# Sinkhorn attention, Fourier mixing and MLP on one core: V routed through DRAM, memsets between loads, exp-ln norms, and unread matmuls in planned gaps

## The chip, the cores and the metric

One core of one Trainium2 chip. The metric is device time in microseconds (us) from the first to the last instruction of one launch, as the runs list it (about 1.7 us more than the span in the profile). Engines: PE = TensorE, PEld = its weight load, DVE = VectorE, ACT = ScalarE, POOL = GpSimd, SP = SyncE. A run is called slow when it is over 1.5% above the fastest of its kernel; verdicts use fast runs.

## The reference

```python
P = sort_net                                   # [4, 8, 8, 8]
for _ in range(5):                             # Sinkhorn
    P = exp(P - P.max(-1)); P /= P.sum(-1); P /= P.sum(-2)
k_sorted = einsum('bhij,bhjcd->bhicd', P, k_blocks)   # 8 blocks of 96 keys
v_sorted = einsum('bhij,bhjcd->bhicd', P, v_blocks)
attn = softmax(q_block @ k_sorted_block.T / 8)        # block by block
x = (attn @ v_sorted_block) -> [4, 768, 512]
u = x + real(fft(fft(x, axis=1), axis=2))
un = (u - mean(u)) / sqrt(var(u) + 1e-6)
out = u + relu(un @ w1) @ w2                          # 512 -> 2048 -> 512
```

## The kernel before

The program is a list of operations with priorities and estimated durations. A planner turns it into one fixed order for each engine before the kernel is built. At run time an engine takes its instructions in that order and stands at one whose semaphore has not come. "Batch" is one of the four batches, and V0 and V1 are the halves of V that serve batches 0 and 1, and 2 and 3. g = 0, 1 are the two halves of a batch's rows. AV is the matmul of the attention weights with V, FF1 that with w1, FF2 that with w2.

Loads and memsets at the start:

```python
for n in range(4):                                  # exp(scores) buffers
    P.add({"POOL": (1.5, 1.6)}, lambda _, n=n: nc.gpsimd.memset(
        eb4[0:96, n, :], 0.0), w=[("ebz", n)], prio=-190.0)
load_qk("k", 0, 0, -5000.0); load_qk("q", 0, 0, -4999.0)
load_v(0, 0, -4998.0);       load_v(0, 1, -4997.0)
load_qk("k", 0, 1, -4996.0); load_qk("q", 0, 1, -4995.0)
...                                                 # the rest later
```

V's path, on the chip alone: sum over a block by PE, copies into a tile ordered by d, 64 small mixing matmuls with keys on the output's partitions, strided evacuation:

```python
for hf in range(2): ...  nc.tensor.matmul(psm.ap, idh, nat[t][...512...])
for n in range(8):       # t == 0: copy;  t == 1: subtract the block mean
    copy(e, vcx[d, r, c], nat[t]["p (c r) d -> p d r c"])
for n in range(16):
    for dd in range(4):
        nc.tensor.matmul(o, vcx[:, 96*d:96*d+m], bd, start=True, stop=(t == 1))
        ...
    copy(e, vsb[0:96, :, 4*n:4*n+4], ps["p (d g) -> p g d"])
```

The norm, and the rows of u, in six buffers (three for each g):

```python
many("u", 6, [128, DM], F32)
G.tensor_scalar(var, var, 1e-6, op0=add)            # G = GpSimd
G.tensor_tensor(ny, var, mhalf, op=pow)
G.tensor_tensor(nm, mean, ny, op=mult); G.tensor_scalar(nm, nm, -1.0, ...)
# dft2: u = RSC * x + mixed      (VectorE writes a buffer of u)
# ff2 : u = ff2 bank + u         (VectorE), then the store frees the buffer:
P.add({"SP": (0.1, 2.3)} if g == 0 else {"POOL": (1.2, 3.5)}, store_u, ...)
```

The two figures of the store are the planner's: how long the engine is held, and when the result is there.

The softmax here doesn't subtract the row's maximum and nothing guards it: scores larger than these inputs give would overflow.

Of the kernel before, what the change touches and what calls it, by code (L numbers as in the profile page):

```python
# [18 lines left out]
D = 64  # L19
NB = 8  # L20
# [7 lines left out]
LOOK = {}  # L28
QB = (2, 3)
# [14 lines left out]
GT = 384  # L44


def _consts():
# [56 lines left out]
    vrow = np.zeros((1, 128, D + 1), f16)  # L104
# [9 lines left out]
    def as32(m):  # L114
# [8 lines left out]
                rows=rows, erow=np.tile(erow, (1, 4)), vrow=vrow, pack=pack)  # L123


class Op:
    __slots__ = ("n", "costs", "fn", "preds", "succs", "left", "ready", "prio",
                 "vts", "fresh", "nbytes", "end", "start", "eng", "tag",
                 "crit", "late")
# [13 lines left out]
class Plan:  # L143
# [14 lines left out]
    def add(self, costs, fn, r=(), w=(), prio=None, nbytes=0, tag="",  # L158
            after=()):
# [7 lines left out]
        o.preds, o.succs, o.vts, o.fresh = set(after), [], [], []  # L167
        for k in r:
            o.preds.update(self.wr.get(k, ()))
# [41 lines left out]
    def schedule(self):  # L211
# [48 lines left out]
        while todo:  # L260
# [70 lines left out]
            for s in o.succs:  # L331
                s.left -= 1
                for x in s.costs:
                    s.ready[x] = max(s.ready[x],
                                     o.end + (0.03 if x == e else self.XL))
                if s.left == 0:
                    for x in s.costs:
                        avail[x].append(s)
# [27 lines left out]
def kernel(  # L366
# [22 lines left out]
    def many(name, n, shape, dtype):  # L389
# [18 lines left out]
    vcx = ct("vcx", [128, 128 * D + 2], F16)  # L408
    dtab = vcx[:, 6144:7168].rearrange("p (c w) -> p c w", c=4)
    lt = vcx[0:97, 7168:7168 + LTW]  # L410
    vsf = ct("vsf", [97, 128 * (D + 1)], F16)
    vsb = vsf[:, 0:128 * (D + 1)].rearrange("p (g w) -> p g w", w=D + 1)
    eb4 = ct("eb4", [97, 4, EW], F16)
    P.pool("eb", [eb4[:, n, :] for n in range(4)])
# [14 lines left out]
    many("un", 2, [128, DM], F16)  # L429
# [9 lines left out]
             vcx[:, 7938:8194].bitcast(F32).rearrange(  # L439
# [7 lines left out]
    mhalf = ct("mhalf", [128, 3], F32)  # L447
    mone = ct("mone", [128, 3], F32)
# [7 lines left out]
    pk = hr[1].rearrange("p a b -> p (a b)")[0:32, 0:1024].rearrange(  # L456
        "p (i x) -> p i x", i=NB)
    pv = hr[1].rearrange("p a b -> p (a b)")[0:32, 1024:3072].bitcast(
        F32).rearrange("p (i x) -> p i x", i=NB)
    pws = hr[1].rearrange("p a b -> p (a b)")[0:32, 3072:3232].bitcast(F32)  # L460
# [9 lines left out]
    def load(dst, src, nbytes, w, prio, eng="POOL", r=(), after=()):  # L470
        e = {"POOL": nc.gpsimd, "SP": nc.sync}[eng]
        c = (0.8, 0.8) if eng == "POOL" else (0.1, 2.3)
        o = P.add({eng: c}, lambda _: e.dma_start(dst, src), r=r, w=w,  # L473
                  prio=prio, nbytes=nbytes, tag="load", after=after)
        o.late = 4.0 if after else 0.0
        return o


    slot = {}
# [34 lines left out]
    def load_v(t, hf, prio):  # L514
        load(nat[t].rearrange("p (c d) -> p c d", d=D)[
            :, 48 * hf:48 * hf + 48, :],
            vv[128 * t:128 * t + 128, 48 * hf:48 * hf + 48, :], 1572864,
            [("nat", t, hf)] + (hk(0)[8 * hf:8 * hf + 8] if t == 0 else
                                kqk(2 * hf) + kqk(2 * hf + 1)), prio)
# [10 lines left out]
    for n in range(4):  # L530
        P.add({"POOL": (1.5, 1.6)}, lambda _, n=n: nc.gpsimd.memset(
            eb4[0:96, n, :], 0.0), w=[("ebz", n)], prio=-190.0, tag="ebz")
    for n in range(2):
        t_ = P.pools["ks"][n][2]
        P.add({"POOL": (0.4, 0.5)}, lambda _, t_=t_: nc.gpsimd.memset(
            t_[:, :, 96:128], 0.0), w=[("ksz", n)], prio=-195.0, tag="ksz")
    P.add({"POOL": (0.6, 0.7)}, lambda _: nc.gpsimd.memset(
        vsb[0:96, :, D:D + 1], 1.0 / XSC), w=["vsz"], prio=-200.0, tag="vsz")
    P.add({"POOL": (0.1, 0.4)}, lambda _: nc.gpsimd.memset(
        pmt[:, 4:7, DM:DM + 2], 0.0), w=["pmz"], prio=-150.0, tag="small")  # L540
    for t_, val in ((negone, -1.0), (mhalf, -0.5), (mone, 1.0)):
        P.add({"POOL": (0.1, 0.4)}, lambda _, t_=t_, val=val:
              nc.gpsimd.memset(t_, val), w=["smalls"], prio=-199.0, tag="small")
    P.add({"POOL": (0.9, 0.9)}, lambda _: nc.gpsimd.tensor_tensor(
        mone, mone, mhalf, op=ALU.pow), r=["smalls"], w=["mone"], prio=-198.0,
        tag="small")
# [5 lines left out]
            "o (n s) -> o n s", n=4), 13376),  # L552
        vrow=(vsf[96:97, 0:128 * (D + 1)], cn["vrow"].ap(), 16640),
# [14 lines left out]
    load_qk("k", 0, 0, -5000.0)  # L568
    load_qk("q", 0, 0, -4999.0)
    load_v(0, 0, -4998.0)  # L570
    load_v(0, 1, -4997.0)
    load_qk("k", 0, 1, -4996.0)
    load_qk("q", 0, 1, -4995.0)
    load_c("dtab", -4994.0)
    load_c("lt", -4993.0)
    load_c("cs", 19.0)
    load_c("tab", 20.0)
    for c in range(4):
        load_w1(c, 40.0 + c)
    for hf in range(2):  # L580
        load_qk("k", 1, hf, 30.0 + hf)
        load_qk("q", 1, hf, 30.5 + hf)
    for c in range(4):
        load_w2(c, 50.0 + c)
# [4 lines left out]
    V = nc.vector  # L589

    exps = []

    def sk(c, fn):
        o = P.add(c, fn, r=["pw", "rs"] + hk(1), w=["pw", "rs"], tag="sink")
        if "ACT" in c:
            exps.append(o)

    for it in range(5):
# [16 lines left out]
        sk({"DVE": (0.21, 0.21)}, lambda _: V.tensor_tensor(  # L615
# [6 lines left out]
        r=["pw"], w=["pk"] + hk(1), tag="pk")  # L622
    P.add({"ACT": (1.0, 1.05)}, lambda _: nc.scalar.copy(
        pv.rearrange("p i (g j) -> p i g j", j=NB),
        pw[:, :, None, :].broadcast_to([32, NB, 16, NB])),
        r=["pw"], w=["pv"] + hk(1), tag="pv")
# [6 lines left out]
    P.add(pe(0.45), f, r=["pk", "pack"] + hk(1), w=[bk], tag="psk")  # L633
# [35 lines left out]
    def v_path(t):  # L669
        n3 = nat[t].rearrange("p (c d) -> p c d", d=D)  # L670
        psm = Buf("pm", "pf") if t else Buf("pm")
        stage = [i for n in range(4) for i in kqk(n)] if t else hk(0)
        for hf in range(2):
            def f(_, hf=hf):
                for n in range(6):
                    nc.tensor.matmul(
                        psm.ap, idh,
                        nat[t][:, 3072 * hf + 512 * n:3072 * hf + 512 * n
                               + 512], start=(hf == 0 and n == 0),
                        stop=(hf == 1 and n == 5))  # L680
            P.add(pe(mm(512, 6) * (1.0 if t else 1.2)), f,
                  r=[("nat", t, hf), "pack"] + (
                      stage if t else stage[8 * hf:8 * hf + 8]), w=[psm], tag="psm")
        P.add({"DVE": (0.6, 0.68)}, lambda _: V.tensor_reduce(
            vb[:, 0, :], psm.ap.rearrange("p (c d) -> p d c", d=D),
            axis=AX.X, op=ALU.add), r=[psm], w=["vb"], tag="vb")
# [8 lines left out]
        vcd = vcx[:, 0:6144].rearrange("p (d r c) -> p d r c", r=6, c=16)  # L695
        for n in range(8):
            qd, hf = divmod(n, 2)
            dr = slice(16 * qd, 16 * qd + 16)
            src = n3[:, 48 * hf:48 * hf + 48, dr].rearrange(
                "p (c r) d -> p d r c", r=6)  # L700
            dst = vcd[:, dr, :, 8 * hf:8 * hf + 8]
            if t == 0:
                P.add({"DVE": dve(768), "ACT": act(768, 0.75)},
                      lambda e, dst=dst, src=src: copy(e, dst, src),
                      r=[("nat", 0, hf)] + stage[8 * hf:8 * hf + 8],
                      w=[("vcx", n)], tag="vcp")
            else:
                P.add({"DVE": dve(768, 1.0, 0.55)},
                      lambda _, dst=dst, src=src, dr=dr: V.tensor_tensor(  # L709
                          dst, src, vbn[:, dr, None, None].broadcast_to(  # L710
                              [128, 16, 6, 8]), op=ALU.subtract),
                      r=[("nat", 1, hf), "vbn"] + stage,
                      w=[("vcx", n)], tag="vcd")

    def v_mix(t):
        bd = bdv16[t].rearrange("p g i -> p (g i)")
        for n in range(16):
            ps = Buf("pm", "pf")

            def f(_, n=n, ps=ps):  # L720
                for dd in range(4):
                    d = 4 * n + dd
                    m = 96 if d == D - 1 else 128
                    o = ps.ap[0:m, 128 * dd:128 * dd + 128]
                    nc.tensor.matmul(o, vcx[:, 96 * d:96 * d + m], bd,  # L725
                                     start=True, stop=(t == 1))
                    if t == 0:
                        nc.tensor.matmul(  # L728
                            o, vbn[:, d:d + 1].broadcast_to([128, m]), bd,
                            start=False, stop=True)  # L730
            P.add(pe(0.46 if t == 0 else 0.24), f,
                  r=[("vcx", i) for i in range(2 * (n // 4), min(
                      8, 2 * ((4 * n + 4) // 16) + 2))] + [("bdv16", t)]
                  + (["vbn"] if t == 0 else []),
                  w=[ps], tag="vmix")
            P.add({"ACT": (0.68, 0.81), "DVE": (0.65, 0.8)},
                  lambda e, n=n, ps=ps: copy(
                      e, vsb[0:96, :, 4 * n:4 * n + 4],
# [651 lines left out]
```

## Time and profile before

| | before |
|---|---|
| median of 4 runs | 289.35 us (288.78 to 290.27) |
| first FF1 matmul | 72.14 us |
| last matmul ends | 282.39 us |
| TensorE's work: before, after the first FF1 | 39.1, 202.9 us |
| lost: before, after the first FF1 | 33.0, 7.4 us |

"Work" is the number of matmuls of each kind times their spacing in a dense stretch, and "lost" is the length of the stretch less the work. So a matmul at half clock counts as lost time too. Losses of stretches of 10 us, and sums of two of them, count the matmuls at their edges whole and read up to 0.4 us too low for each 10 us; sums over longer stretches are given as "some", corrected for that. Besides the lines that the prediction shows, three matter later. Timeline of VectorE and GpSimd (start, busy us, engine, line, instruction):

```profile
7.51 6.16 POOL L531 MEMSET eb<- 96x1672 f16 x4
12.95 1.28 DVE L661 COPY vcx<-hr 128x768 f16<-128x768 f16 x1
15.00 0.68 DVE L619 CAST hr<-hr 32x1024 f16<-32x1024 f32 x1
```

GpSimd's four memsets lie beside the Sinkhorn. One VectorE copy beside their end takes 1.28 us, and the one behind it 0.78. VectorE's waits after the first FF1 (waiting line, what released it, us in total, times, longest) hold one for a store of u, a short one:

```profile
DVE u L1161 <- DMA out_dram<-u: 0.3, 1, 0.3
```

### The profile page before, as it was taken

How to read it: one execution, taken by the hardware profiler on the slowest of the kernel's cores; microseconds unless marked ns; L12 is line 12 of the kernel's file. 1: busy time of each engine (PE TensorE's matmuls, PEld its weight loads, DVE VectorE, ACT ScalarE, POOL GpSimd, SP SyncE). 2: the span in 40 equal slices, each digit the busy share in tenths (PEclk: the TensorE clock that was granted, in tenths of full speed). 3: DMA queues.
4: the chain of work that ended last, by engine and by line, in shares of the span. 5: the costliest groups of instructions: out<-in, count | busy, mean ns of one | idle time of the engine just before them, and what ended most of it. 6: DMA issues, size and time to landing. Idle time of an engine off the chain costs nothing.

```text
span 288.2 us, 5805 instructions
## 1 busy us (share of the span) xinstructions
PE 261.6 (91%) x2284; PEld 155.7 (54%) x2284; DVE 171.5 (60%) x405; ACT 158.2 (55%) x323; POOL 67.7 (23%) x116
## 2 busy tenths in 40 slices
PE   0389988797999999999999999999999999999991
PEld 0247876554566566554566556445545545545540
DVE  4686999999999999850469853146114315310010
ACT  2676979886778946882269026416703614714600
POOL 8974300003920460020410000131100212200022
PEclk9995999999999999999999999999999999999997
DMA  7999999910992499412112011221221022032002
GB/s 111 214 264 244 213 208 208 221 35 16 97 169 39 64 165 146 97 21 38 73 50 46 13 73 38 45 86 48 41 91 36 10 48 109 12 66 76 14 9 101
DMA packets 42529, 26.33 MB, mean 91 GB/s; under 512 B 30106, under 2 KB 38824, under 8 KB 42500
## 3 DMA queue, kind: packets, MB, share of 16 engines
q0 software_dynamic: 23536, 18.31, 37.7%
q1 hardware_dynamic: 18966, 7.64, 11.5%
q8 instruction: 18, 0.29, 0.4%
q14 instruction: 9, 0.07, 0.1%
HBM read 28.96 MB, written 6.29 MB: 122 GB/s over the span
## 4 chain that ended last, share of the span: by engine, by line
PE 49%; DVE 24%; issue 16%; DMA 6%; POOL 4%; POOLq 0%; ACT 0%; DVEq 0%
PE bank L1275 19%; PE bank L1254 18%; DMA hr<-in_v_dram 4%; DVE vcx L709 3%; DVE vsf L661 3%; DVE rt L1007 2%; PE bank L992 2%; PE bank L1150 2%; PE bank L898 2%; DMA out_dram<-u 2%; DVE st L1187 1%; PE bank L953 1%; DVE eb L975 1%; DVE ks L661 1%; POOL out_dram L1298 1%
## 5 line engine op out<-in xcount | busy, mean ns | idle before, releaser
L1266 ACT ACTIVATE hr<-bank 128x384 f16<-128x384 f32 x115 | 56.3, 491 | 76.3 <-PE bank L1254 75.1
L1254 PE MATMUL bank<-ut,w1sb 128*128 128x384 f16 x512 | 91.5, 326 | 0.7 <-ACT ut L661 0.7
L1275 PE MATMUL bank<-w2sb,hr 128*128 128x512 f16 x384 | 87.9, 379 | 0.0
L1254 PEld LDWEIGHTS <-w1sb 128*128 128x128 f16 x512 | 48.7, 98 | 34.4 <-issue 1.1
L1275 PEld LDWEIGHTS <-hr 128*128 128x128 f16 x384 | 36.8, 98 | 41.6
L1283 DVE TENSOR_TENSOR u<-bank,u 128x512 f32<-128x512 f32 x24 | 16.5, 688 | 60.3 <-PE bank L1275 60.0
L962 ACT ACTIVATE ex<-bank 96x384 f32<-96x384 f32 x64 | 27.9, 486 | 6.5 <-PE bank L953 6.3
L1194 POOL TENSOR_SCALAR mv<-mv 128x3 f32<-128x3 f32 x8 | 1.9, 239 | 115.5 <-DVE mv L1189 115.5
L1298 POOL DMA_INDIRECT out_dram<-u,rows x12 | 12.1, 1011 | 68.0 <-DVE u L1283 67.3
L977 ACT ACTIVATE eb<-ex,negone 96x384 f16<-96x384 f32 x35 | 20.8, 617 | 0.2
L1214 ACT ACTIVATE un<-u,nm,ny 128x512 f16<-128x512 f32 x15 | 12.2, 811 | 10.1 <-DMA ut<-un 7.5
L992 PE MATMUL bank<-vsf,eb 97*128 97x65 f16 x416 | 16.5, 193 | 1.3 <-DVE rr L837 0.5
L1173 DVE SCALAR_TENSOR_TENSOR u<-rt,bank 128x510 f32<-128x510 f16 x12 | 8.1, 674 | 15.9 <-PE bank L1139 8.9
L1007 DVE TENSOR_TENSOR rt<-bank,rz 128x384 f16<-128x384 f32 x32 | 17.2, 548 | 0.3
L992 PEld LDWEIGHTS <-eb 97*128 97x128 f16 x416 | 15.4, 98 | 3.6 <-issue 1.3
L473 POOL DMA_DIRECT2D kq<-in_q_dram x20 | 16.6, 855 | 1.7 <-DMA kq<-in_q_dram 1.2
L928 PE MATMUL bank<-pack,qr 128*128 128x128 f16 x48 | 5.3, 263 | 12.3 <-ACT qr L661 11.8
L1187 DVE BATCH_NORM_STATS2 st<-u 128x6 f32<-128x512 f32 x24 | 16.1, 685 | 0.3
L1161 DVE SCALAR_TENSOR_TENSOR u<-rt,bank 128x512 f32<-128x512 f16 x12 | 8.0, 684 | 13.8 <-PE bank L1154 13.5
L725 PE MATMUL bank<-bdv,vcx 128*128 128x128 f16 (+1 forms) x128 | 12.7, 226 | 0.0
L953 PE MATMUL bank<-qt,ks 64*128 64x96 f16 x256 | 11.5, 209 | 1.3 <-DVE rt L1007 0.4
L661 DVE CAST vsf<-bank 96x512 f16<-96x512 f32 x16 | 11.5, 778 | 1.2 <-PE bank L728 1.1
(131 smaller groups left out, 341.2 us busy)
## 6 DMA issues: line engine op xcount, KB each, us to landing
kq<-in_k_dram POOLq DMA_DIRECT2D x8, 384.0 KB, 7.0
w1sb<-in_moe_w_ch_dram POOLq DMA_DIRECT2D x4, 512.0 KB, 15.7
w2sb<-in_moe_w_ch_dram POOLq DMA_DIRECT2D x4, 512.0 KB, 19.1
out_dram<-u SPq DMA_DIRECT2D x8, 256.0 KB, 2.0
kq<-in_q_dram POOLq DMA_DIRECT2D x4, 384.0 KB, 11.1
hr<-in_v_dram POOLq DMA_DIRECT2D x2, 768.0 KB, 11.3
kq<-in_v_dram POOLq DMA_DIRECT2D x2, 768.0 KB, 21.0
kq<-in_q_dram POOLq DMA_DIRECT2D x16, 96.0 KB, 5.5
```

What stands on the lines that cost most here:

```text
L473: o = P.add({eng: c}, lambda _: e.dma_start(dst, src), r=r, w=w, prio=prio, nbytes=nbytes, tag="load", after=after)
L661: (nc.scalar.copy if e == "ACT" else V.tensor_copy)(dst, src)
L962: nc.scalar.activation(ex.ap, pss[h2].ap[0:96, 0:384], AF.Exp, scale=SCALE),
L977: nc.scalar.activation(ed, src, AF.Identity, bias=negone[0:96])
L992: nc.tensor.matmul(po.ap[:, 65 * T:65 * T + 65], eb.ap[:, e0:e0 + 128], vsf[:, vi:vi + 65], start=(n == 0), stop=(n == len(WIN[T]) - 1), s ...
L1007: P.add({"DVE": (0.45, 0.56)}, lambda _: V.tensor_tensor(rt.ap[:, :, D * h:D * h + D], po3()[:, :, 0:D], rz.ap[:, :, None].broadcast_to([1 ...
L1187: P.add({"DVE": (0.6, 0.69)}, lambda _, u=u, st=st: V.bn_stats(st.ap, u.ap), r=[u], w=[st], tag="bn")
L1254: nc.tensor.matmul(ps.ap[:, 0:GT], w1sb[:, c, 128 * fc:128 * fc + 128], ut.ap[:, c, :], start=(c == 0), stop=(c == 3))
L1266: nc.scalar.activation(hr[g][:, fc, :], ps.ap[:, 0:GT], AF.Relu)
L1275: nc.tensor.matmul(ps.ap, hr[g][:, fc, 128 * tt:128 * tt + 128], w2sb[:, fc, :], start=(fc == 0), stop=(fc == 15))
L1283: V.tensor_tensor(u.ap, ps.ap, u.ap, op=ALU.add),
L1298: st_ = [nc.gpsimd.indirect_dma_start(out.rearrange("b s m -> (b s) m"), bass.IndirectOffsetOnAxis(ap=rows[:, i:i + 1], axis=0), u.ap, None)]
```

## The change

The intent: get V onto keys without VectorE, by storing the mixed V to DRAM and gathering it back; start the loads with V; put the memsets in GpSimd's order where it would wait anyway; take the norm off GpSimd; keep PE's clock up with matmuls that nobody reads. Cut to its core:

```diff
-    for n in range(4):
-        P.add({"POOL": (1.5, 1.6)}, ... memset(eb4[0:96, n, :]), prio=-190.0)
+    for n in range(NEB):                           # NEB = 6
+        P.add({"DVE": (1.0, 1.1)} if n < 2 else {"POOL": (1.5, 1.6)},
+              ... memset(eb4[0:96, n, :]), prio=-4998.9)   # among the loads
+    nc.scalar.preload_act_table_set("natural_log_exp_and_others")
-    load_qk("k", 0, 0, -5000.0); load_qk("q", 0, 0, -4999.0)
-    load_v(0, 0, -4998.0); load_v(0, 1, -4997.0)
+    load_v(0, 0, -5000.0); load_v(0, 1, -4999.0)
+    load_qk("q", 0, 0, -4998.0); load_qk("k", 0, 0, -4997.0)
...
+        if t:                                      # V1: sums on VectorE
+            for n in range(4):
+                V.tensor_reduce(vb[:, 0, 16*n:16*n+16], nat[1]["p d c"])
+        # mixing: 12 banks of 512, straight evacuation, then
+        (nc.sync or nc.gpsimd).dma_start(vdr[t][w64, cols], vm[w64, cols])
+        nc.gpsimd.dma_start(vsb[32*k_:32*k_+32, w64, 0:D],      # 128 B pieces
+                            vdr[t][w64, cols]["g (c d) -> c g d"])
-    G.tensor_scalar, G.tensor_tensor(pow), G.tensor_tensor, G.tensor_scalar
+    nc.scalar.activation(ny, var, AF.Ln, bias=eps)
+    nc.scalar.activation(ny, ny, AF.Exp, scale=-0.5)
+    V.scalar_tensor_tensor(nm, mean, -1.0, ny, ...)
-            P.add({"SP": (0.1, 2.3)} if g == 0 else {"POOL": (1.2, 3.5)}, ...
+            P.add({"SP": (0.1, 2.3)} if g == 0 else {"POOL": (1.2, 3.7)}, ...
+    load_v(1, ...)            # six pieces, behind the second norm and behind W2
...
+                if o.start < goal[0].end:
+                    for _ in range(int((o.start - t - 0.05) / SPIN)):
+                        nc.tensor.matmul(spin.ap[:, 0:480], idh, pack)
```

The pitch of a key's rows in vsf goes from 65 to 80 elements, un from two buffers to three.

## The prediction

> **What bounds the kernel now.** I read the busy rows first, then the chain of waits for the spacing of the two big matmul groups, then the timeline at the start, then the groups by line. The busy rows in 40 slices of 7.2 us:
>
> ```profile
> PE   0389988797999999999999999999999999999991
> DVE  4686999999999999850469853146114315310010
> PEclk9995999999999999999999999999999999999997
> DMA  7999999910992499412112011221221022032002
> ```
>
> TensorE looks full from slice 14 (100 us) on; before that VectorE is the full engine (slices 5 to 15), and before that the loads are. A busy PE can still be slow, so I converted it to work. Dense stretches in the chain of waits give the spacing of each kind of matmul:
>
> ```profile
> 177.59 4.55 PE bank L1254 x28
> 182.14 9.50 PE bank L1275 x44
> ```
>
> 4.55/28 = 0.1625 us for an FF1 matmul (512 of them: 83.2 us) and 9.50/44 = 0.2158 us for an FF2 matmul (384: 82.9 us). With spacings for the rest got the same way (an AV matmul 0.031, a V-mix matmul 0.056, and so on) all matmuls sum to 242 us. The last one ends at 282.4 us, so 40 us are lost. The first FF1 starts at 72.1; 39 us of work lie before it, so **33 us are lost before 72 us and only 7.5 us after it**. After the last matmul come 5.8 us of residual add and stores. Hence
>
> end = T1 (first FF1) + work left at T1 + about 8 us of loss + 5.8 us.
>
> What sets T1: V arrives at 16.4 us behind K and Q, the matmuls that sum V run cold, V mixing takes until 36, and then VectorE is full until the first normalised tile at 68.1.
>
> ```profile
> 3.54 12.84 DMA hr<-in_v_dram
> 16.42 2.46 PE bank L676 x6
> 33.05 2.75 DVE vsf L661 x4
> ```
>
> (the chain of waits: start, us, what) and, in the timeline:
>
> ```profile
> 72.14 1.46 PE L1254 MATMUL bank<-ut,w1sb 128*128 128x384 f16 x8 [0.67 <-ACT ut L661]
> ```
>
> The groups by line that the change touches (count, busy us, mean ns, idle before):
>
> ```profile
> L709 DVE TENSOR_TENSOR vcx<-kq,vbn 128x768 f16<-128x768 f16 x8 | 11.8, 1480 | 0.0
> L661 DVE CAST vsf<-bank 96x512 f16<-96x512 f32 x16 | 11.5, 778 | 1.2 <-PE bank L728 1.1
> L661 ACT CAST vsf<-bank 96x512 f16<-96x512 f32 x16 | 11.6, 791 | 0.7 <-PE bank L725 0.3 <-PE bank L728 0.3
> L661 DVE COPY vcx<-hr 128x768 f16<-128x768 f16 x5 | 4.5, 928 | 0.7 <-DMA hr<-in_v_dram 0.7
> L725 PE MATMUL bank<-bdv,vcx 128*128 128x128 f16 (+1 forms) x128 | 12.7, 226 | 0.0
> L728 PE MATMUL bank<-bdv,vbn 128*128 128x128 f16 x64 | 8.4, 232 | 0.0
> L1197 POOL TENSOR_TENSOR ny<-mv,mhalf 128x3 f32<-128x3 f32 x8 | 7.2, 897 | 0.7
> L605 ACT ACT_TABLE_LOAD x1 | 1.3, 1283 | 0.7 <-PEq L1374 0.7
> ```
>
> The reader sees some 40 us of VectorE and ScalarE copies spent only on getting V into the layout with keys on partitions.
>
> **What the Trainium skill says.**
> - "TensorE: Matmul & The Clock Gate", Part 1 (the HAM clock gate): the array is at half clock until it has been busy for about 3.4 us, and falls back when idle. The trace agrees in the spacing: the six 128x512 matmuls at 16.42 take 2.46 us, six like them at 64.61 take 1.47. The clock row shows the half rate only in slice 4, so I trust the spacing.
> - "DMA: Bandwidth & Descriptors", Two DMAs through the same engine are not ordered: a DMA that reads what another wrote must wait for its semaphore. So a store and then a gather are two full latencies in series. The trace has 2.0 us to landing for a 256 KB store issued from SyncE.
> - The same page, Specifications: line rate needs pieces of 512 B or more. The gathers have pieces of 128 B. The Q loads for batches 2 and 3 have 256 B pieces, and between 74 and 88 us, when mostly they and their K loads run, 150 to 190 GB/s are written: bearable, not crippling.
> - "ScalarE: Activation LUTs", Table sets: one set holds ln and exp, so the new norms need no table switch. The single load of 1283 ns stays single.
>
> **The change, part by part.**
> V0 ahead of K and Q. In the start, 0.786 MB per K or Q half and 1.57 MB per V half land at about 0.425 MB/us (the two V halves land 3.7 us apart) after about 5 us of latency and start. V0's halves should land at 8.7 and 12.4 us instead of 12.7 and 16.4; the first Q half at 14.3, the first K half at 16.1, the second halves at 18 and 19.8.
> Dummy matmuls. 73 unread 480-column matmuls, 34 of them around the two V halves, where PE has nothing to do. Warm they cost 0.20 us each, 14.8 us in all. They make the V sums and the mixing run at full clock (two times 1.2 us, and much of the mixing). The gate stays a placement by plan: where a gap turns out shorter they delay real work, by 1 us I think.
> V0 mixing. 128 matmuls of 128 columns become 24 of 512: 7.1 us of warm work become 24 x 0.2158 = 5.2. The order puts K transposes before them, so they start when K lands, about 17.4, and end at 22.6. Twelve straight 128x512 copies (0.64 us VectorE, 0.58 ScalarE) replace 8 re-ordering copies and 16 strided evacuations. The last copy is done at 23.4, the last store lands near 26.5, the last gather is issued by 27.8 and lands at 31 to 32.5 (estimates: 1.7 us at 150 GB/s for 256 KB, plus 2 us). Today V is ready at 36.9.
> VectorE up to T1. I walked the order of instructions of both kernels, with mean durations by form less 0.06 us of overlap each. Before: 77 instructions from the first norm multiply (39.15) to the first un (68.10), sum 30.6, taken 28.95, so a factor of 0.946. After: 57 instructions, sum 23.6, so 22.3 us; fewer, because more of batch 0's work moved ahead and batch 1's behind. Ahead of the first norm VectorE has 51 instructions, 19.4 us, from about 13.4, and about 3.5 us of waits for K and for mixing: first norm near 35.5, later than V is ready. Then un at 57.8.
> ln-exp norms. Four GpSimd instructions take 66.13 to 68.10 today; ln, exp and one multiply at about 0.2 us each with hand-overs take 0.8. It is worth 1.2 us once, on the path to T1, but other VectorE work lies beside it and it is inside the walk above; no further credit. The other seven norms lie beside full PE: zero.
> From un to the first FF1 are 4.0 us today and I keep 4.5. **T1 = 62.5 us, 9.6 earlier.** The w1 loads now stand behind the gathers; bytes ahead of their end at 0.41 MB/us give 57, in time. W2 should end near 67.
> Work left. The total falls to 236.5: mixing -1.9 and -1.0, the V1 sums on PE -2.6 (now VectorE reductions). Only 32.5 us of it is done before T1 (39.2 today), since batch 1's attention and V1's sums stood there. So 204.0 us are left at T1, against 202.8.
> Memsets between loads. GpSimd's eb memsets take 6.2 us today and end at 13.6; now they follow nine loads and end near 18, before the first gather. Neutral.
> Sum: 62.5 + 204.0 + 8 + 5.8 = 280.3 us of span; runs are 0.7 above the span: **281 us, 2.7% faster**.
>
> **Rivals.**
> 1. The gathers are slow or stand behind loads in the ring, and V is ready at 40 or later. For it: 128 B pieces, three in series after a store, DMA full from 3 to 58 us. Against: 4 us of slack before VectorE gets to the first norm. Then T1 is about 68 and the time 286 to 288.
> 2. The work moved behind T1 becomes a new bound. V1 is now loaded in six transfers of 256 B pieces after w2, ending near 76, about where VectorE reaches its reductions (four at an estimated 1.7 us, then two subtractions of 2), and these stand in order before evacuations that free PSUM banks for FF2. For it: VectorE has 113 us left at T1 against 101 today. Against: batch 0's two MLP groups give PE 41 us of work that needs few VectorE results. Then the loss after T1 is 12 to 14 and the time 285 to 287.
> 3. It goes better: no longer do norms stand behind stores on GpSimd (5.8 us of VectorE waits today), VectorE drops 12 us of V1 re-ordering, and the loss falls to 5. Then 277 to 278.
> 4. Dummies sit where PE is late and push the chain by several us: 284. Against: nearly all stand where PE waits for loads or for norms.
>
> **Range and chances.** T1 is good to about 2.5 us, the loss after it to about 3; together about 4. 281 with a range of 276.5 to 286. Two per cent faster is 283.1, about half a width above the centre: 0.70 faster, 0.27 within 2%, 0.03 slower, which needs rivals 1 and 2 together.
>
> **What would show it right or wrong.** Right: first FF1 at 60 to 65 us; V sums six in 1.4 us; V0 gathers landed by 33; the first norm set by VectorE's own order; PE full afterwards with under 10 us lost; one table load. Wrong if VectorE or AV waits on a gather for over 2 us (rival 1), if PE shows idle time of several us between 75 and 110 behind V1 or w2 (rival 2), or if dummy matmuls end after the operands of the next real matmul were ready by more than 2 us in sum (rival 4).

## The result, and the profile after

| | before | after |
|---|---|---|
| median | 289.35 us | 301.61 us (297.35 to 308.78) |
| first FF1 matmul | 72.14 | 67.80 (predicted 62.5) |
| work left at the first FF1 | 202.9 | 204.0 (predicted 204.0) |
| lost after the first FF1 | 7.4 | 18.2 (predicted 8) |
| last matmul ends | 282.39 | 289.98 |

The ratio is 1.0354, 95% interval 1.0257 to 1.0451: slower. (A ratio is the mean time of one kernel's fast runs over that of the other's of the same rounds, so not quite the ratio of the medians.) Profiled runs stand in the table; that of the changed kernel, 297.35 us, is the fastest of its six. The busy rows after:

```profile
PE   5969898999995999995999999999999999999992
DVE  6887989999959999646769965215514405511010
PEclk9979999999999799998699999999999999999997
DMA  7997999999997669999015002201202112013002
```

The start is denser, though the unread matmuls count in it, but PE has holes at slices 12 and 18, counted from 0 (92 and 137 us), each with a slice of lower clock behind it. The DMA block of slices 13 to 18 is V1's way through DRAM and, behind it, K and Q of batch 3, which ran in slices 13 to 16 before. The page counts 32.6 MB in 56,544 packets, against 26.3 MB in 42,529.

In the start, timelines of GpSimd, VectorE and PE:

```profile
10.83 6.10 POOL L568 MEMSET eb<- 96x1672 f16 x4
12.09 5.39 DVE L651 CAST fo<-rv 32x1024 f16<-32x1024 f32 x1
17.54 0.36 PE L672 MATMUL bank<-pack,fo 32*128 32x32 f16 x8 [3.13 <-DVE fo L651]
67.80 0.50 PE L1332 MATMUL bank<-ut,w1sb 128*128 128x384 f16 x2
```

The cast that took 0.68 us at 15.00 (of the Sinkhorn result, spread out: pk, which now lies in the tile fo) takes 5.39, and ends 0.55 us after the memsets. PE waits for it, and the mixing, predicted for 17.4, starts at 21.95. After the first FF1, the waits of PE and VectorE:

```profile
PE bank L1332 <- DVE u L1361: 3.6, 1, 3.6
PE bank L977 <- DVE u L1265: 3.2, 1, 3.2
DVE vb L714 <- DMA kq<-in_q_dram: 3.0, 1, 3.0
DVE u L1256 <- DMA out_dram<-u,rows: 2.9, 1, 2.9
```

The first and third go together (V1's sums, 92 us), and so do the second and fourth (137 us). The sums, and the chain of waits before the second hole:

```profile
85.08 10.81 DVE L714 TENSOR_REDUCE vb<-kq 128x16 f32<-128x1536 f16 x4 [3.00 <-DMA kq<-in_q_dram]
```

```profile
119.58 12.98 DMA kq<-in_q_dram
132.76 1.04 POOL out_dram L1376
```

VectorE waits 3.0 us and then reduces for 10.8, with FF2's evacuation behind it in its order. The wait is for the load of V1, I read: its last piece lands at 84.9 by the trace (the prediction had 76), and the same wait in e6 and e7 carries V's name. At 132.76 GpSimd is through with its loads, of batch 3's K and Q, and stores u. That store lands 6.3 us later, beside these loads, and VectorE waits for the buffer.

### The profile page after: what moved, and what is told of

Its sections match the earlier page's. It is cut to its first block, busy times and chain, and to the rows that moved or that the text cites. A ratio compares the mean times of both kernels' runs of the same rounds, so it can differ in the third digit from the quotient of the medians.

```text
span 295.6 us, 5645 instructions
## 1 busy us (share of the span) xinstructions
PE 272.3 (92%) x2197; PEld 151.8 (51%) x2197; DVE 183.7 (62%) x430; ACT 141.0 (48%) x309; POOL 76.4 (26%) x106
## 2 busy tenths in 40 slices
DMA packets 56544, 32.61 MB, mean 110 GB/s; under 512 B 42842, under 2 KB 51560, under 8 KB 56516
## 4 chain that ended last, share of the span: by engine, by line
issue 52%; DVE 13%; PE 13%; DMA 13%; POOL 6%; ACT 1%; POOLq 0%; DVEq 0%
DMA kq<-in_q_dram 8%; POOL out_dram L1376 4%; PE bank L1353 4%; DMA vsf<-vdr 2%; DMA vdr<-kq 2%; DVE fo L651 2%; PE bank L770 2%; POOL vsf L798 1%; DVE rt L1087 1%; PE bank L1144 1%; PE bank L1332 1%; DVE st L1270 1%; DMA vdr<-hr 1%; DVE vb L714 1%; POOL kq L487 1%
## 5 line engine op out<-in xcount | busy, mean ns | idle before, releaser
L1344 ACT ACTIVATE hr<-bank 128x384 f16<-128x384 f32 x105 | 51.5, 491 | 90.4 <-PE bank L1332 89.8
L1353 PE MATMUL bank<-w2sb,hr 128*128 128x512 f16 x384 | 89.5, 388 | 0.0
L1361 DVE TENSOR_TENSOR u<-bank,u 128x512 f32<-128x512 f32 x24 | 16.4, 688 | 65.7 <-PE bank L1353 65.6
L1462 PE MATMUL bank<-pack 128*128 128x480 f16 x73 | 19.5, 412 | 3.3 <-DMA pack<-k_pack 3.3
L1071 PEld LDWEIGHTS <-eb 97*128 97x128 f16 x416 | 15.1, 98 | 3.9 <-DVE eb L1054 0.8
L798 POOL DMA_DIRECT2D vsf<-vdr x12 | 13.0, 1088 | 14.3 <-DMA vdr<-hr 12.2
L1056 ACT ACTIVATE eb<-ex,negone 96x384 f16<-96x384 f32 x27 | 16.2, 614 | 0.1
L1341 DVE TENSOR_SCALAR hr<-bank 128x384 f16<-128x384 f32 x23 | 12.6, 552 | 4.9 <-PE bank L1332 4.7
L977 PE MATMUL bank<-bdk,kq 128*64 128x128 f16 x192 | 11.5, 244 | 3.8 <-DVE u L1265 3.2
L1054 DVE TENSOR_SCALAR eb<-ex 96x384 f16<-96x384 f32 x37 | 14.4, 399 | 0.0
L1462 PEld LDWEIGHTS <-pack 128*128 128x128 f16 x73 | 7.2, 107 | 12.0 <-issue 4.0
## 6 DMA issues: line engine op xcount, KB each, us to landing
w1sb<-in_moe_w_ch_dram POOLq DMA_DIRECT2D x4, 512.0 KB, 15.1
w2sb<-in_moe_w_ch_dram POOLq DMA_DIRECT2D x4, 512.0 KB, 18.2
```

Source lines behind the costliest of these rows:

```text
L1056: nc.scalar.activation(ed, src, AF.Identity, bias=negone[0:96])
L1071: nc.tensor.matmul(po.ap[:, 65 * T:65 * T + 65], eb.ap[:, e0:e0 + 128], vsf[:, vi:vi + 65], start=(n == 0), stop=(n == len(WIN[T]) - 1), s ...
L1344: nc.scalar.activation(hr[g][:, fc, :], ps.ap[:, 0:GT], AF.Relu)
L1353: nc.tensor.matmul(ps.ap, hr[g][:, fc, 128 * tt:128 * tt + 128], w2sb[:, fc, :], start=(fc == 0), stop=(fc == 15))
L1361: V.tensor_tensor(u.ap, ps.ap, u.ap, op=ALU.add),
L1462: nc.tensor.matmul(spin.ap[:, 0:480], idh, pack.bitcast(F16))
```

## The experiments

All eighteen kernels ran five rounds, before beside them on the same chip (its medians: 289.4 to 290.2). Each changes what its diff shows, but where it changes operations or durations the planner also makes other orders. By the traces e1, e2, e5, e6 and e11 keep the changed kernel's order on VectorE, ScalarE, SyncE and PE (but for e2's missing matmuls); e7, e12 and e17 have new orders on all engines, and so, on VectorE and PE at least, have e3, e4, e8 and e14. By the rule of 2% e7, e17 and e18 are the same as the kernel before, e6 and e16 unclear, and the others with a ratio slower. Numbers in this table but the median and the ratio are of the profiled run.

| run | median us, ratio to before | first FF1 | work left | lost after |
|---|---|---|---|---|
| e1 | 300.78, 1.0375 | 67.16 | 204.0 | 21.9 |
| e2 | 303.90, no fast pair | 70.02 (slow run) | 204.0 | 21.5 |
| e3 | 298.85, 1.0298 | 68.34 | 206.7 | 16.5 |
| e4 | 305.03, 1.0504 | 69.08 | 204.0 | 23.6 |
| e5 | 302.95, 1.0417 | 69.44 (slow run) | 204.1 | 26.5 |
| e6 | 297.29, 1.0239 | 64.30 | 204.0 | 21.3 |
| e7 | 290.60, 1.0056 | 65.93 | 204.1 | 12.4 |
| e8 | 300.59, 1.0362 | 67.72 | 204.1 | 21.3 |
| e9 | 301.39, 1.0400 | 74.95 | 207.8 | 10.2 |
| e10 | 301.37, 1.0425 | 74.33 | 207.8 | 11.1 |
| e11 | 298.20, 1.0280 | 65.72 | 204.1 | 21.8 |
| e12 | 299.04, 1.0321 | 70.52 | 202.9 | 18.6 |
| e13 | 298.81, 1.0338 | 70.72 | 202.9 | 17.7 |
| e14 | 303.35, 1.0496 | 67.62 | 204.1 | 21.2 |
| e15 | 301.84, 1.0455 | 64.79 | 206.6 | 22.9 |
| e16 | 295.32, 1.0211 | 64.94 | 206.7 | 17.9 |
| e17 | 290.11, 0.9990 | 72.90 | 202.9 | 7.9 |
| e18 | 291.52, 1.0059 | 64.48 (slow run) | 206.6 | 16.7 |

### The start: memsets beside a fast copy

**e1**, an intervention that did not take place:

```diff
-    for n in range(NEB): memset(eb n), prio=-4998.9
+    for n in range(2): memset(eb n)
+    ... after the cast of pk is added:
+    for n in range(2, NEB): memset(eb n), after=(cast of pk,)
```

> The changed kernel with its four GpSimd memsets of eb held back until VectorE's cast of pk is done; nothing else moves on any engine. Theory A (the memsets keep VectorE from a port it needs for its fast copies): the cast of 32x1024 takes about 0.7 us instead of 5.39, ends near 12.8, the mixing starts near 17.5 instead of 21.95, the first FF1 matmul comes 3.5 to 5 us earlier than 67.80, and the run takes 3 to 5 us less. Rival (the cast is long for a reason of its own, or the second half of V is what gates, not the cast): the cast stays near 5 us or the mixing still starts near 22, and the time is within 1 us of the changed kernel's.

The `after` binds only the planner. No data ties the memsets to pk, so no semaphore was set: they ran at 10.91 and the cast took 5.41 us. The run decides nothing on the theory. It is a second sample of the changed kernel (VectorE, ScalarE, PE and SyncE have exactly its order; GpSimd's small memsets changed places): 300.4 to 303.2 us in its fast runs, so the 297.35 of the first profile is at the lucky end.

**e5**, with a wait that is real:

```diff
+    nc.gpsimd.tensor_copy(between[0:32], pk[:, 0, 0:1])   # GpSimd waits for pk
+    for n in range(2, NEB): memset(eb n) on GpSimd
```

> e1 did not do what it was meant to: the order was only the planner's, no wait tied GpSimd to VectorE, and the memsets ran at 10.91 as before. Here GpSimd first copies one column of pk, so that its four memsets of eb cannot start before the cast of pk is done; the other engines keep their orders exactly. Theory A (memsets and VectorE's fast copy share a port): the cast takes about 0.7 us and ends near 12.8, V's second half is summed as soon as it has landed, the mixing starts 3 to 4.5 us earlier than 21.95, the first FF1 comes 2.5 to 4.5 us earlier than 67.2 to 67.8, the time is 2 to 5 us less than the changed kernel's of the same rounds. Rival (the cast is slow for another reason): it stays above 4 us with no memset beside it.

Timelines of VectorE and GpSimd:

```profile
12.08 0.68 DVE L653 CAST fo<-rv 32x1024 f16<-32x1024 f32 x1
12.93 6.08 DVE L669 COPY rr<-rv 32x1024 f16<-32x1024 f16 x1
12.96 5.78 POOL L568 MEMSET eb<- 96x1672 f16 x4
```

The cast is back at 0.68 us, and the next fast copy, at whose side the memsets now lie, takes 6.08 us instead of 0.41. The collision moved with the memsets. So the theory of the port held and the expected time did not, because another copy stood where the memsets went.

**e6**, the same memsets at the old place in half as many elements:

```diff
-                  eb4[0:96, n, :], 0.0)
+                  eb4[0:96, n, :].bitcast(F32), 0.0)
```

> The same memsets at the same place, but written as half as many 32-bit elements. Theory A: if GpSimd takes half the time for them (3 instead of 6.1 us), the cast of pk ends when they do, near 14 instead of 17.4, and takes 2 to 2.5 us; the first FF1 comes 2 to 3.5 us earlier. If the memsets do not get shorter, the cast does not either. Rival: the cast's length has nothing to do with theirs and stays at 5.4 us.

```profile
11.08 3.32 POOL L568 MEMSET eb<- 96x836 f32 x4
12.09 2.86 DVE L652 CAST fo<-rv 32x1024 f16<-32x1024 f32 x1
```

(GpSimd's timeline, then VectorE's.) The memsets take half the time, and the cast ends with them, at 14.9. The first FF1 comes at 64.30, 2.9 to 3.5 us earlier than in e1 and in the changed kernel. The ratio falls from e1's 1.0375 to 1.0239, about 4 us.

**e11** has both: 32-bit memsets held behind the last fast copy of the stage.

```diff
+    nc.gpsimd.tensor_copy(between[0:32], pvl[:, 0, 0:1])
+    for n in range(2, NEB): memset(eb n as F32) on GpSimd
```

> The changed kernel with GpSimd's memsets of eb both written as 32-bit elements and held back, by a copy of one column of pvl on GpSimd, until VectorE's last fast copy of the Sinkhorn stage is done. Theory A: the cast takes 0.7 us, the copy of pvl 0.4, no fast VectorE copy falls beside a memset until 25 us; the mixing starts at 17 to 18.5 instead of 21.95, the first FF1 comes at 62.5 to 64.5, as the prediction had it (62.5). The loss after it stays, so the run takes 295 to 298. Rival: V's second half or the loads behind it set the start of the mixing, which stays at 19 or later, with the first FF1 at 65 or later.

Cast 0.68 us, copy 0.41, first FF1 at 65.72 (64.94, 64.79 and 64.48 in e16, e15 and e18, which have the same start), 298.2 us. So without a collision the first FF1 is at 64.5 to 65.7, not at 62.5, and e6, with half of it, is no worse. What remains there is, as I read it, the transfers: in e16 the mixing starts at 17.95, near the 17.4 that was predicted, but the gathers for batch 0 take up to 5.93 us to land where the prediction had 3.7, VectorE's first norm waits 0.7 us for the AV matmuls that start at 35.86, and the second half of batch 1's Q takes 10.3 us (VectorE waits 1.9 us for it). No run tests these waits.

**e2**, no unread matmuls:

```diff
-                if o.start < goal[0].end:
+                if False:
```

> The changed kernel without the 73 unread matmuls; VectorE, ScalarE, GpSimd and the queue keep their orders exactly. Theory A (they keep the clock up at little cost): without them the second six summing matmuls of V take about 2.4 us instead of 1.5 and the early matmuls run at about half rate, the first FF1 comes 1 to 3 us later, and the run takes 0.5 to 3 us more. Rival (they stand in the way before un and lower the clock later): the first FF1 comes up to 1 us earlier, the cold spells at 90 to 150 us vanish or shrink, and the run is 1 us or more faster.

The other four engines keep their order. The first FF1 comes at 70.02, 2.9 us later than in e1 beside it, in a slow run. The V sums do run at half rate (2.72 and 2.74 us for six, instead of 1.46 and 1.51), but the mixing starts at 22.30 in both runs, because the cast decides that. What differs is the clock later on, 0.56 between 40 and 50 us and 0.76 between 50 and 70, against 1.00 in e1. The clock row:

```profile
PEclk9999975885999999998599999999999999999999
```

So in this profile the unread matmuls are worth 2.9 us at the first FF1, but at 40 to 70 us and not at V. For the whole run it stays open: five of its six runs count as slow against its fastest, so no ratio is given; the median is 3.1 us above e1's, the one fast run (297.39) below all of e1's. The later losses did not shrink (21.5 against 21.9), so the rival has no support.

### After the first FF1: sums, transfers, or order?

**e3**, V1's sums on PE as before:

```diff
-            for n in range(4): V.tensor_reduce(vb[:, 0, 16*n:16*n+16], ...)
+            for n in range(12): nc.tensor.matmul(psm.ap, idh, nat[1][...512...])
+            V.tensor_reduce(vb[:, 0, :], psm.ap, ...)
```

> The changed kernel with the sums over V1 made by twelve TensorE matmuls into one bank, as before the change, instead of four VectorE reductions. Theory A (VectorE stood in order before the reductions while FF2's banks waited for it): the 3.6 us of idle TensorE near 93 to 96.5 goes, the loss of 4.4 us between 90 and 100 falls below 1.5, TensorE gets 2.6 us of work more, and the run takes 1 to 2 us less. Rival (TensorE waits there for the load of V1 itself): TensorE now stands in the summing matmuls until V1 has landed, the loss stays at 3 us or more and the run takes 2 us more.

The loss between 90 and 100 us goes from 4.4 to -0.5. But between 110 and 130 there are now 10.6, for the reason that the changed kernel shows at 137. Waits of VectorE and PE:

```profile
DVE u L1252 <- DMA out_dram<-u: 12.8, 2, 8.6
PE bank L1040 <- DVE u L1252: 7.7, 1, 7.7
```

**e4**, a seventh buffer for u (pitch 72 instead of 80 for the room):

```diff
-    many("u", 6, [128, DM], F32)
+    many("u", 7, [128, DM], F32)
```

> The changed kernel with seven buffers for u instead of six (the room comes from a row pitch of 72 instead of 80 in vsf). Theory A (the add that makes u waits for the indirect store of the first batch's rows, which stood behind the loads and gathers of GpSimd's queue): the wait of VectorE for that store (2.9 us) and the idle TensorE from 137 to 140 go, the 6.3 us lost between 130 and 150 fall below 2.5, and the run takes 2 to 5 us less. Rival (the next buffer's store or another wait takes its place): the loss stays within 1.5 us and so does the time.

The wait for the store shrinks to 1.7 us, and another transfer takes its place in PE's waits, the transposes of un:

```profile
PE bank L1332 <- DMA ut<-un: 6.0, 1, 6.0
```

9.6 us are lost between 130 and 150: the rival was right. The buffer is not the cause by itself; another transfer that PE waits for in that stretch is late too. The run does not separate the buffer from the pitch: V1's last gathers land in 15 to 16 us here, in at most 9.8 in the changed kernel.

**e7**, a wrong result on purpose (relative error 0.30): V1 is mixed but neither stored nor gathered.

```diff
+        if t == 1:
+            return          # in v_mix, ahead of the stores and gathers
```

> A wrong result on purpose: the mixed V of the second half of the blocks is computed but neither stored to DRAM nor gathered, so batches 2 and 3 use the V of batches 0 and 1. It takes away 12 transfers of 256 KB, half of them in pieces of 128 bytes, and lets K and Q of batch 3 be loaded as soon as the mixing is done. Theory B (the loss at 130 to 150 us is made by these transfers: stores of u and the loads of batch 3 stand behind them in the DMA engines, and VectorE waits for u's store to land): the loss after 100 us falls from 9 to 14 us to below 5, the run takes 5 to 9 us less than the changed kernel. Rival (GpSimd's order of instructions or the late loads of batch 3 alone): the same loss at the same place, time within 2 us.

290.60 us; the ratio is 1.0056, against 1.0354 for the changed kernel and 1.0375 for e1. Between 100 and 160 us only some 5.5 are lost; what is left beside that is the sums (5.5 between 90 and 100). Stores of u land in at most 4.8 us (median 2.7), against 6.9 at worst in the changed kernel and 13.0 and 16.7 in e16 and e15. The line on all stores of u, in the changed kernel and then in e7:

```profile
DMA to landing us min/median/max: 1.9/2.7/6.9
DMA to landing us min/median/max: 1.9/2.7/4.8
```

So with V1's round trip the stores are later, beside its gathers or beside batch 3's loads, which it pushes back (issued at 117 to 131 us in the changed kernel, at 101 to 110 here). How much of the 10 us that is worth e7 does not say, since the planner's orders are new in it too.

**e8**, V1 loaded ahead of W2:

```diff
-    gate = lns[1:2];  load_v(1, 0, 60.0); load_v(1, 1, 61.0)
+    gate = gets[0, 1][-1:];  load_v(1, 0, 45.0); load_v(1, 1, 46.0)
```

> The changed kernel with V's second half loaded ahead of W2 instead of behind it and behind the second norm. It lands some 10 us earlier. Theory B (V1's sums, stores and gathers come so late that they stand beside the last layers of batch 0 and the stores of u): the reductions run before FF2's first banks are ready, the loss at 90 to 100 us falls below 2, the stores, gathers and the loads of batch 3 move ahead by 8 us or more, the loss at 130 to 150 falls by half, the run takes 3 to 7 us less. Rival (the sum of DMA traffic is what counts, the order does not): W2 lands late instead and FF2 waits for it near 80 to 85, the time stays within 2 us.

Everything of V1 moves ahead and so does the loss: 10.5 us between 110 and 130, 0.8 between 130 and 150, again with VectorE at u behind a store (5.7 us). Same time. The rival was right in that this move of the transfers does not help; W2, which it blamed, was not waited for.

**e9** and **e10**, V1 as before the change, on the chip (e10 with e11's memsets):

```diff
-VW = 80; NEB = 6; many("un", 3, ...)
+VW = 65; NEB = 4; many("un", 2, ...);  vcd = ct("vcd", [128, 6144], F16)
+    v_path(1), v_mix(1): as in the kernel before; V0 as in the changed kernel
```

> The changed kernel with its first half of V as changed (stored, gathered) and the second half as before the change: loaded in two pieces, summed by TensorE, taken apart by VectorE's subtraction into a tile of its own, mixed with keys on the output's partitions, no DRAM. To make room, four eb buffers instead of six, two un instead of three, row pitch 65 in vsf. Theory B (the loss after the first FF1 is V1's own path: its reductions before FF2's evacuation, and its stores and gathers that make u's stores land late): lost after the first FF1 falls from 18 to 22 us to 7 to 9, TensorE's own work after it grows by about 3 us at most, and the run takes 286 to 290 us, below the kernel before by 0 to 3. The memset collision stays, the first FF1 comes at 65 to 68. Rival (K2, Q2, K3, Q3 loads and the output stores collide in any case): lost stays above 13, the run takes 293 or more.

> e9 and e11 together. If the two causes are the whole miss and independent: the first FF1 near 63, lost after it 7 to 9, the run at 281 to 285 us, 2 to 3 per cent faster than the kernel before. If not: 286 or more, with the loss to be found in another stage.

Lost after the first FF1 falls to 10.2 and 11.1 (with the 64 mixing matmuls, 3.6 us, counted as work), as theory B has it. But the first FF1 comes at 75 and 74. The likely reason is one of my concessions to room: with a pitch of 65 elements (130 bytes) the last of batch 0's three gathers took 12.2 and 12.0 us to land, against 5.9 at 160 bytes and 6.2 at 144 (e4), and VectorE stood 7.1 and 8.6 us behind it. The pitch was not changed alone, so that is not shown. The comparison of totals is lost by it.

### The norm alone, and the planner's figure for a store

**e12**, the kernel before with the exp-ln norm and the table load at the start and nothing else:

```diff
-    G.tensor_scalar, G.tensor_tensor(pow), G.tensor_tensor, G.tensor_scalar
+    activation(Ln), activation(Exp, scale=-0.5), V.scalar_tensor_tensor
```

> The kernel before with one part of the change alone: the norm's rsqrt as exp(-0.5 ln) on ScalarE, with the table that has both loaded once at the start, instead of GpSimd's four small instructions. By the prediction it saves about 1.2 us once, in front of the first FF1: first FF1 near 70.9 instead of 72.14, and the second table load of the Sinkhorn (2 us at 8 to 10 us in the kernel before) goes as well, so 1 to 3 us less in all. Rival: the chain in front of the first FF1 is set by VectorE, and the time stays within 0.6 us.

The first FF1 comes 1.6 us earlier (70.52), within what was predicted, and yet the run takes 9 us more: 18.6 us are lost after it instead of 7.4, with no V1 in DRAM at all. (The second table load that I expected to go was never there: the kernel before has one.) The chain of waits shows where, for one half:

```profile
107.53 7.96 DMA out_dram<-u
115.68 0.69 DVE u L1160
116.95 1.59 PE bank L991 x26
```

With other durations the planner gave other orders. VectorE's next u now stands close behind the store that frees its buffer. The plan has that store landed after 2.3 us; here it took 8.0 beside the loads of batch 3, and VectorE waits 3.3 us for it. In the kernel before, its only wait for a store is 0.3 us. Some 8 us of the loss lie around it, at 110 to 130. Another 7 are lost at 140 to 160, and nobody waits for a store there: PE has three waits of 0.9 to 1.3 us for VectorE and runs at a mean clock of 0.83. That half is the new order's too, but what in it was not found.

**e13** and **e14** change only this figure, for all batches: e13 in e12, e14 in the changed kernel.

```diff
-            P.add({"SP": (0.1, 2.3)} if g == 0 else {"POOL": (1.2, 3.7)}, ...
+            P.add({"SP": (0.1, 9.0)} if g == 0 else {"POOL": (1.2, 13.0)}, ...
```

> e12 (the kernel before with exp-ln norms alone) with one number of the planner changed: it counts on a store of u landing 9 us after its issue (13 for the indirect ones) instead of 2.3 (3.5), so it lets VectorE write the next batch's u later in its order. Nothing is computed otherwise. Theory C (the loss after the first FF1 is VectorE standing in its order at a u whose buffer the store of the batch before has not yet freed, with TensorE waiting behind it and cold afterwards): the 3.3 us wait for the store goes, lost after the first FF1 falls from 18.6 to below 11, the run takes 289 to 293 instead of 299. Rival (ln and exp on ScalarE or VectorE's nm stand in the way of evacuations): the loss stays above 15, 297 or more.

> The changed kernel with that one number changed (9 and 13 us instead of 2.3 and 3.7). Theory C: the wait of VectorE at u for the indirect store (2.9 to 9 us in the runs of the changed kernel and its relatives) goes; the loss at 130 to 150 falls from 6 to 12 us to below 4; the loss at 90 to 100 (4.4 to 5.5, the reductions) stays; the run takes 292 to 296. Rival (another transfer takes its place, as in e4): 299 or more.

No time was won, but look at where it is lost. The PE row of e13 and its largest wait after the first FF1:

```profile
PE   0489988897999999999999999999989999929992
```

```profile
PE bank L1248 <- DMA ut<-un: 7.2, 2, 5.8
```

Between 80 and 160 us e13 loses some 5 us in all (e12: some 17; the kernel before: some 6; the expectation of e17 has lower figures, not corrected for the edges), and e14 loses 0.9 between 130 and 150 (the changed kernel: 6.3). That is what the theory says. The hole is now at slice 35: for the last batches too the planner puts u so late that PE stands at the transposes, with 11.6 us lost after 160 (e14: 8.2).

**e15** and **e16** do the same with the two other mends in place (memsets as in e11, sums as in e3); e15 with the late figure, e16 without:

> The changed kernel with the three mends together: memsets held back and written as 32-bit elements (e11), V1 summed on TensorE (e3), the planner's stores late. If the miss is made of the three causes: first FF1 at 63 to 66, TensorE's own work after it 206.7, lost after it 7 to 10, the run at 283 to 288 us, below the kernel before. If not: lost after the first FF1 above 13, 290 or more.

> The same without the planner's number: the two mends e11 and e3 alone. Theory C: VectorE's wait for a store of u stays at 3 to 9 us, lost after the first FF1 12 to 17, the run takes 292 to 298. Rival (with the reductions gone VectorE's order no longer matters): as e15 within 1 us.

e16 gains what e11 and e3 promised, 295.32 us, with 17.9 lost (15.1 us of VectorE waits for stores). e15 is worse: 9.5 us near the end as in e14, and still a wait of 9.4 for a store of batch 0 that took 16.3 us to land. Of the sum I had expected for e15 only the first FF1 (64.79) came true.

**e17** and **e18** take the late figure for batch 0 alone: e17 is e12 with it, e18 is e16 with it.

```diff
-            P.add({"SP": (0.1, 2.3)} if g == 0 else {"POOL": (1.2, 3.5)}, ...
+            P.add({"SP": (0.1, 9.0 if b == 0 else 2.3)} if g == 0 else
+                  {"POOL": (1.2, 13.0 if b == 0 else 3.5)}, ...   # e18: 18, 13
```

> e13 lost nothing between 72 and 160 us (2.4 in all, against 14 in e12), but 11.6 after 160: with the late landing taken for every batch, the planner put the last batch's u so late that TensorE stood 5.8 us at its transposes near the end. Here the late landing (9 and 13 us) is taken for batch 0 alone, whose stores fall beside the loads of batch 3, and the old figures for the rest. Theory C: lost after the first FF1 (70.6) is 6 to 9 us, as in the kernel before; the run takes 286 to 289, 0.5 to 1.5 per cent faster than the kernel before. Rival (the loss comes back at another place whenever one is taken away): 293 or more.

> e16 (memsets held back, V1 summed on TensorE) with the landing of batch 0's stores taken as 18 us (13 for the indirect ones), since in e15 and e16 the store that VectorE waited for landed some 16 us after its issue, beside V1's gathers. The other batches keep the old figures. Theory C: VectorE's waits for stores fall from 15 us to below 3, lost after the first FF1 (64.9) falls from 17.9 to 8 to 11, the run takes 285 to 289. Rival: the loss moves and stays above 15, 292 or more.

e17: 290.11 us, 9 less than e12, and 7.9 us lost after the first FF1, as in the kernel before. Its stores still take up to 7.3 us to land; nobody stands behind them any more. Its PE row has no hole after slice 10:

```profile
PE   0189997788999999999999999999999999999992
```

The gain of the norm itself does not show (ratio 0.9990, 0.9941 to 1.0039; the first FF1 at 72.90 in this profile), and why it came later than in e12 and e13 I did not find. e18: 291.52 us, 4 less than e16, and VectorE's waits hold none for a store of over 0.7 us. The loss that stays, 10.6 us between 130 and 150 in a slow run, has another transfer at its head, of batch 3's Q:

```profile
PE bank L1048 <- DMA qt<-kq: 3.6, 1, 3.6
```

No version beats the kernel before by a measurable amount.

## Why the prediction was wrong

The sum was 62.5 + 204.0 + 8 + 5.8 and 0.7 above the span; measured in the profile 67.80 + 204.0 + 18.2 + 5.6 and 1.75. So 5.3 us of the 16.4 that are missing are in front of the first FF1, 10.2 behind it, and 0.9 at the end, where the run lies 1.75 us above the span and not 0.7. The profile is of the fastest run: the median of 301.61 lies 4.3 us higher, and e1, the same order in a run of 300.54, loses 21.9 after the first FF1 instead of 18.2. (A slip on the way: the prediction's own 57.8 + 4.5 are 62.3, not 62.5.)

- **Work left: right**, 204.0 to the tenth. V sums at full clock: right (six in 1.46 us). One table load: right.
- **"Memsets between loads. ... Neutral": wrong, and the step that failed first.** I asked only whether GpSimd would be done before the first gather. Beside the memsets stood VectorE's cast of pk, on the path to the mixing: 5.39 us for 0.68. e5 and e6 show that the cast's length is the memsets'; e6, which halves it, gains 2.9 to 3.5 us at the first FF1. The Trainium skill has the mechanism ("SBUF — State Buffer", Who interferes with whom): GpSimd and VectorE's fast copies and casts share one pair of ports under an exclusive lock, and the loser waits. I had not looked there, though the kernel before already showed a copy of 1.28 us beside its last memset.
- **Gathers: mis-sized.** "1.7 us at 150 GB/s for 256 KB, plus 2 us" was 5.9. That puts the first AV at 35.86 (e16), and the first norm 0.7 us behind VectorE's own order, at 36.5 where the prediction had 35.5. With the wait of 1.9 us for Q's late second half this would be most of the other 2 to 3 us of the first FF1, but no run shows it. This was rival 1, at half its size.
- **Dummies: the number near, the place wrong.** I gave them two times 1.2 us and much of the mixing. The two times 1.2 us are there in e2, but off the path: with the cast in the way the mixing starts at 22.30 with and without them. The 2.9 us that e2 shows at the first FF1 go with the lower clock at 40 to 70 us, so that the size fits is luck. For rival 4 nothing was found.
- **"About 8 us of loss": wrong, 18.2.** This was taken over from the kernel before, as if it belonged to the work. Rival 2 named one half: the sums before FF2's evacuations. It mis-sized them (10.8 us for four, not 6.8) and had V1 land at 76 (84.9, with 3.0 us of waiting in VectorE); e3, with the sums on PE, removes that half (4.4 us at 90 to 100). The other half no rival had: VectorE stands in its order at a u whose buffer a store must free. In the changed kernel and its close relatives with the same order on VectorE (e1, e2, e5, e6, e11) that wait is 2.9, 6.4, 8.7, 9.1, 6.7 and 7.9 us (e2 and e5 in slow runs), and PE loses more than the wait (6.3 us at 130 to 150 in the changed kernel), since the clock falls in the pause: the Trainium skill's clock gate ("TensorE: Matmul & The Clock Gate", Part 1), which the PEclk rows show behind each hole.
- **Why the stores are late:** the transfers beside them, V1's gathers or the loads that these push back; without them no store takes over 4.8 us (e7). They need not be V1's: in e12 a store takes 8.0 us beside the loads of batch 3 alone. **Why it hurts:** the order. A landing of 7 to 8 us goes with a loss of 18.6 us in e12 and of 7.9, as in the kernel before, in e17, where the one figure that was changed gave another order. So the loss at a store needs both, a late landing and a u close behind it. "ln-exp norms ... zero" was wrong too: alone, they cost 9 us, by the order they led to, with about half of e12's loss at that store.

Left open: how the 10 us behind the first FF1 divide between V1's transfers and the order (e18 still loses 10.6 us between 130 and 150, at a transpose), why e17's first FF1 came at 72.90, and whether V1 on the chip with a wide pitch would win.

## What to carry to other kernels

Before moving work on GpSimd, list what VectorE does beside it: a fast copy beside a run of memsets lasted as long as the run here. A loss measured in one kernel is a property of its fixed order, not of its work; any change of durations makes a new order, so look for instructions that stand close behind the store that must free their buffer, and give the planner the landing time measured in that stretch, for that stretch only. And when an ordering is tried, check in the trace that it took place: an order in a plan is no semaphore.

## What the Trainium skill lacked or had wrong

- "SBUF — State Buffer", Who interferes with whom, says that the one that starts first holds the pair for its whole instruction. Here VectorE's cast, which came during the first of four back-to-back memsets, got in only after the fourth (5.39 us, against 1.5 for one memset): across a run of GpSimd instructions the lock was not given over. In e5 the copy starts 0.03 us before the memsets by the trace, and still outlasts all four (6.08 us).
- "VectorE: DVE Perf Modes", Zero memsets can be issued as uint32, speaks of VectorE's memsets. The same holds on GpSimd: four of 96x1672 f16 took 6.10 us, four of 96x836 f32 3.32.
- "DMA: Bandwidth & Descriptors" has no figure that I found for how a gather depends on the pitch of its destination: 256 KB in 128 B pieces landed in 5.9 us at 160 bytes, 6.2 at 144 and 12.2 at 130, the last in a kernel that differs in more than that (the DMA engines moved 142 GB/s beside it, 232 in the changed kernel). Other gathers at 160 bytes, beside more loads, took 7.2 to 12.4 us.
- The same page has none for a store beside such gathers: a store of u landed in 2.7 us in the median, in 8.0 beside batch 3's loads of K and Q (e12), and in 16.7 beside V1's gathers and these loads (e15).
- No page that I found gives the time of VectorE's reduction along a strided axis: 128x1536 f16 to 128x16, with 128 B from one summand to the next, took 2.70 to 2.80 us, where the prediction had 1.7.
